# VectorE's part of a cached-attention decode kernel written as a loop over heads, with an alternating 0 or 1 in place of an odd/even branch

## The chip, the cores and the metric

One core of a Trainium2 chip. The metric is the device time of one execution in microseconds (us), the median of several runs. The engines are PE (TensorE), DVE (VectorE), ACT (ScalarE), POOL (GpSimd) and SP (SyncE); 16 DMA engines, over which the profile's page counts the shares of its queues, move the data. Three words are used throughout: a load *lands* when its data is complete; a *relay* is GpSimd waiting for a load and then raising a semaphore for another engine; the *chain* is the profile's path of work and waits followed back from the last instruction of the program.

## The reference, cut to what matters

One decode step: layernorm, attention of one query over a cache of 32768 keys for each of 32 heads, output projection, then a small MLP.

```
B, Sq, D = 1, 1, 640
H, Sk, Dh = 32, 32768, 192                       # k_cache, v_cache: bf16
q = (x @ wq).reshape(B, Sq, H, Dh)               # one row per head
scores = einsum("bhqd,bhkd->bhqk", q, k_cache) * Dh ** -0.5
o = einsum("bhqk,bhkd->bhqd", softmax(scores), v_cache)
h = x + o.reshape(B, Sq, H * Dh) @ wo
out = h + relu(layernorm(h) @ w1) @ w2
```

K and V together are 805 MB and are read once. Everything else is small.

## The kernel before

It has no scheduler: each engine's program is written out by hand. A class `Program` plans every semaphore count first, and then emits instructions and waits. SyncE issues the loads. A head's K and V come in four tiles each of 3072 KB; K tiles have four buffers, V tiles two.

```
for h in range(H):                                   # dma_program, on SyncE
    for ld in range(NL if h < LAST else NL - 1):
        load(kt[ld][:], rows(k_hd, h, ...), f"dk{ld}", "k", h, ld)
        if n >= NV:
            g.wait("PV", hp, 2 * lp + 1)             # the V tile two before is used up
        load(vt[ld % NV][:], rows(v_hd, h, ...), f"dv{ld % NV}", "v", h, ld)
        ...                                          # wq every 8 heads, wo every 2
```

PE computes most scores of a tile and the value products; DVE computes the scores of 28 of every 64 rows of a partition by multiplying and reducing, and normalizes each head. PE and ACT already execute heads 1 to 30 as a loop (their semaphores are counted down by one head's amount at the end of a turn, so that a turn's waits are constants). DVE's program is written out for all heads, because odd and even heads differ:

```
def o_scale(g, h):                                   # head h goes to row h % 2 of the pair
    g.wait("PV", h, len(chunks(h)) - 1)
    g.wait("rec", h)
    g.do(lambda: dve.tensor_scalar_mul(out=o_pair[:, :, h % 2, :], in0=o_ps[...], scalar1=rec[0:2, 1:2]), ...)

def o_turned(g, h):                                  # only an odd head's oT (the pair) is projected
    g.wait("oT", h)
    if h % 2 == 1:
        g.do(lambda: dve.tensor_copy(out=oT[:], in_=mm[:, 0:3]), "dve_pe", ("oTc", h))
    else:
        g.do(lambda: dve.memset(oT[:], 0.0), "dve_pe", ("oTc", h))

for h in range(H):                                   # dve_program
    for c in range(len(chunks(h))):
        scores_dve(g, h, c)
        if c == 0 and h > 0:
            den_rec(g, h - 1)
            o_scale(g, h - 1)
        if c == 1 and h > 0:
            o_turned(g, h - 1)
```

The softmax here doesn't subtract the row's maximum and nothing guards it: scores larger than these inputs give would overflow.

## Time and profile before

| | before |
|---|---|
| time, median | 1926.88 us of 3 runs |
| data read | 824.97 MB |
| instructions built for DVE / GpSimd | 981 / 352 |

The prediction below shows the lines on which it rests. The row of data rates is to be read beside them, one number for each fortieth of the span, in GB/s:

```profile
GB/s 408 430 432 433 433 432 432 433 433 431 433 430 433 433 433 433 433 432 427 434 433 433 433 431 433 430 435 432 430 431 431 435 432 433 431 431 429 431 432 321
```

The rate is flat, at 427 to 435, from the second slice to the last but one.

### The profile page before, as it was taken

To read this page: it belongs to the slowest core of one execution; us is meant where nothing else is said; L and a number is where in the kernel's file an instruction comes from. 1 tells how busy PE (TensorE), PEld (TensorE's weight loads), DVE (VectorE), ACT (ScalarE), POOL (GpSimd) and SP (SyncE) were. 2 spreads that over 40 slices of the span, in tenths; PEclk is the share of its full clock that TensorE was granted. 3 is DMA by queue.
4 is the path that set the end of the run, shared out by engine and by line. 5 is a ranking of instruction groups with operands and counts; after the bars stand their busy time and mean duration, and the time that the engine had idled before them with its cause. 6 is when DMAs were issued, how large, how long until landed. Compare 5 with 4: busy or idle time off the path is not lost.

```text
span 1925.6 us, 36082 instructions
## 1 busy us (share of the span) xinstructions
PE 1563.4 (81%) x15899; PEld 1074.8 (56%) x15899; DVE 1546.3 (80%) x670; ACT 970.6 (50%) x2031; POOL 0.7 (0%) x6
## 2 busy tenths in 40 slices
PE   5887888787887888788788878888778888888788
PEld 4555555555555555555555555555555555555555
DVE  5888888787887888887788878888778887888786
ACT  4554555454554554555454554545445454545554
POOL 0000000000000000000000000000000000000000
PEclk8889888888989898888888888888888888898888
DMA  9999999999999999999999999999999999999997
GB/s 408 430 432 433 433 432 432 433 433 431 433 430 433 433 433 433 433 432 427 434 433 433 433 431 433 430 435 432 430 431 431 435 432 433 431 431 429 431 432 321
DMA packets 44799, 825.31 MB, mean 429 GB/s; under 512 B 4580, under 2 KB 6116, under 8 KB 12132
## 3 DMA queue, kind: packets, MB, share of 16 engines
q1 hardware_dynamic: 44762, 824.99, 99.8%
q8 instruction: 12, 0.20, 0.0%
q14 instruction: 15, 0.12, 0.0%
q10 hardware_dynamic: 10, 0.00, 0.0%
HBM read 824.97 MB, written 0.00 MB: 428 GB/s over the span
## 4 chain that ended last, share of the span: by engine, by line
DMA 76%; PE 22%; SPq 1%; issue 0%; ACT 0%; POOLq 0%; DVE 0%
DMA kt<-in_A_k_cache_dram 76%; PE o_ps L319 11%; PE tp L338 10%; SPq L221 1%; PE mm L319 1%; PE sp L319 0%; PE attT L319 0%; ACT kT L533 0%; POOLq L301 0%; DVE o_pair L631 0%; ACT pB L539 0%; PE mm L522 0%; ACT h1T L595 0%; DVE y_row L699 0%; DVE h_col L681 0%
## 5 line engine op out<-in xcount | busy, mean ns | idle before, releaser
L617 DVE TENSOR_TENSOR pr<-kt,qb 128x2304 f32<-128x2304 bf16 (+2 forms) x257 | 755.8, 2941 | 298.9 <-DMA kt<-in_A_k_cache_dram 282.6
L533 ACT COPY kT<-tp 128x1024 bf16<-128x1024 bf16 (+1 forms) x899 | 818.9, 992 | 342.2 <-PE tp L338 340.2
L338 PE MATMUL tp<-ident_f,kt 128*128 128x128 f32 x3459 | 571.7, 332 | 341.8 <-POOLq L301 341.8
L620 DVE TENSOR_REDUCE sc<-pr 128x12 f32<-128x2304 f32 (+2 forms) x257 | 755.3, 2939 | 8.9
L338 PEld LDWEIGHTS tp<-ident_f,kt 128*128 128x128 f32 x3459 | 498.1, 173 | 358.7 <-POOLq L301 357.5
L319 PE MATMUL o_ps<-vt,pB 128*2 128x384 bf16 x2286 | 470.9, 357 | 3.5 <-POOLq L301 3.4
L319 PE MATMUL o_ps<-vt,pA 128*2 128x384 bf16 x1778 | 331.0, 326 | 0.0
L319 PEld LDWEIGHTS o_ps<-vt,pB 128*2 128x2 bf16 x2286 | 184.1, 89 | 239.8 <-issue 87.6
L539 ACT ACTIVATE pB<-sp 128x20 bf16<-128x20 f32 (+2 forms) x258 | 47.9, 186 | 503.1 <-PE sp L319 503.1
L319 PEld LDWEIGHTS sp<-qm,kT 128*128 128x128 bf16 x6918 | 193.2, 97 | 77.7 <-issue 67.5
L319 PEld LDWEIGHTS o_ps<-vt,pA 128*2 128x2 bf16 x1778 | 151.0, 85 | 144.7 <-issue 8.1
L319 PE MATMUL sp<-qm,kT 128*128 128x2 bf16 x6918 | 212.0, 164 | 3.0 <-ACT kT L533 2.1
L548 ACT ACTIVATE pA<-sc 128x12 bf16<-128x12 f32 (+2 forms) x257 | 53.4, 208 | 89.0 <-DVEq L64 88.3
L539 ACT ACTIVATION_READ_ACCUMULATOR pB<-sp 128x1 f32 x258 | 50.2, 195 | 0.0
L548 ACT ACTIVATION_READ_ACCUMULATOR pA<-sc 128x1 f32 x257 | 48.7, 190 | 0.0
L625 DVE TENSOR_REDUCE rec<-mm 128x1 f32<-128x20 f32 x32 | 5.7, 179 | 51.6 <-PE mm L319 51.1
L319 PE MATMUL mm<-wq_s,xn_ln 128*1 (+1 forms) x160 | 18.7, 248 | 3.6 <-POOLq L301 3.6
L631 DVE TENSOR_SCALAR o_pair<-o_ps,rec 2x384 bf16<-2x384 f32 x32 | 19.4, 605 | 2.8 <-PE o_ps L319 1.7
L319 PE MATMUL attT<-oT,wo_s 128*128 128x1 bf16 x465 | 15.9, 163 | 0.3 <-DVE oT L638 0.3
L319 PEld LDWEIGHTS mm<-dsums,ones_mat 128*128 128x128 f32 x64 | 9.5, 188 | 10.7 <-issue 9.3
L319 PE MATMUL mm<-ones_row,row_e 1*128 1x1 bf16 x384 | 14.0, 159 | 0.0
L319 PEld LDWEIGHTS attT<-oT,wo_s 128*128 128x128 bf16 x465 | 13.8, 95 | 0.3 <-DVE oT L638 0.3
(69 smaller groups left out, 129.1 us busy)
## 6 DMA issues: line engine op xcount, KB each, us to landing
kt<-in_A_k_cache_dram SPq DMA_DIRECT2D x127, 3072.0 KB, 22.5
vt<-in_A_v_cache_dram SPq DMA_DIRECT2D x127, 3072.0 KB, 15.5
wq_s<-in_A_wq_dram SPq DMA_DIRECT2D x4, 1920.0 KB, 21.9
wo_s<-in_A_wo_dram SPq DMA_DIRECT2D x16, 480.0 KB, 16.3
kt<-in_A_k_cache_dram SPq DMA_DIRECT2D x1, 1920.0 KB, 19.7
kt<-in_A_v_cache_dram SPq DMA_DIRECT2D x2, 960.0 KB, 24.3
kt<-in_B_w_dram SPq DMA_DIRECT2D x1, 1920.0 KB, 18.3
wq_s<-in_B_w_dram SPq DMA_DIRECT2D x1, 960.0 KB, 20.3
```

Source lines behind the costliest of these rows:

```text
L221: g.do(lambda: nc.sync.dma_start(out=dst, in_=src), sem, label, by=16)
L319: return lambda: pe.matmul(o, lhsT=w, rhs=r, **kw)
L338: calls.append(lambda b=b, o=o: pe.transpose(out=dst[:, b, :], in_=src[:, o:o + 2 * P].bitcast(f32), identity=ident_f[:]))
L533: g.do(lambda: act.copy(out=kT[c % 2][:, b0:b0 + nb, :], in_=src[:, 0:nb, :].bitcast(bf16)), "act_pe", ("cp", h, c, k))
L539: g.do(lambda: act.activation(out=pB[c % 4][:, 0:jp], in_=sp[:, 0:jp], func=F.Exp, scale=SCALE, accum_out=dsums[:, 2 * c + 1:2 * c + 2]), ...
L548: g.do(lambda: act.activation(out=pA[c % 4][:, 0:jd], in_=sc[c % NC][:, 0:jd], func=F.Exp, scale=SCALE, accum_out=dsums[:, 2 * c:2 * c + 1 ...
L617: g.chain(lambda: dve.tensor_tensor(out=pr[:, 0:j1 - j0, :], in0=src[:, (off + j0) * Dh:(off + j1) * Dh].rearrange("p (j d) -> p j d", d=D ...
L620: g.chain(lambda: dve.reduce_sum(out=sc[c % NC][:, j0:j1], in_=pr[:, 0:j1 - j0, :], axis=X), "dve")
L625: g.chain(lambda: dve.reduce_sum(out=rec[:, 0:1], in_=mm[:, 0:2 * NCM], axis=X), "dve")
L631: g.do(lambda: dve.tensor_scalar_mul(out=o_pair[:, :, h % 2, :], in0=o_ps[0:2, 0:2 * Dh].rearrange("q (i d) -> q i d", i=2), scalar1=rec[0 ...
```

## The change

Its intent: VectorE, too, runs heads 1 to 30 as one loop. For that all heads must be alike. The new head always goes to row 1 of the pair, the old row 1 is copied to row 0 afterwards, and oT is always written, scaled by `odd`, which flips between 0 and 1. To count waits per turn, DVE no longer waits on a DMA's semaphore or on PE's general one: GpSimd relays each K tile to DVE as well, and PE counts what DVE waits for on a semaphore of its own. The core of the diff:

```diff
-        g.wait("k", h, ld)
+        if h == LAST and ld >= NL - 1:
+            g.wait("k", h, ld)
+        else:
+            g.wait("atd", "k", h, ld)
...
                 relay(g, "k", h, ld)
+                g.do(lambda: nc.gpsimd.sem_inc(sems["pool_dve"], 1))
+                book_relay(g, "k", h, ld, sem="pool_dve")
...
-        g.do(lambda: dve.tensor_scalar_mul(out=o_pair[:, :, h % 2, :],
+        g.do(lambda: dve.tensor_scalar_mul(out=o_pair[:, :, 1, :],
...
     def o_turned(g, h):
+        g.chain(lambda: dve.tensor_scalar(out=odd[:], in0=odd[:], scalar1=-1.0, scalar2=1.0, op0=A.mult, op1=A.add),
+                "dve", ("odd", h))
         g.wait("oT", h)
-        if h % 2 == 1:
-            g.do(lambda: dve.tensor_copy(out=oT[:], in_=mm[:, 0:3]), "dve_pe", ("oTc", h))
-        else:
-            g.do(lambda: dve.memset(oT[:], 0.0), "dve_pe", ("oTc", h))
+        g.wait("odd", h)
+        g.do(lambda: dve.tensor_scalar_mul(out=oT[:], in0=mm[:, 0:3], scalar1=odd[:]), "dve_pe", ("oTc", h))
+        if h < LAST:
+            g.chain(lambda: dve.tensor_copy(out=o_pair[:, :, 0, :], in_=o_pair[:, :, 1, :]), "dve")
...
-            dve_program(Program(book, sems, nc.vector))
+            looped("dve", nc.vector)
```

More of the change, by code (lines that the diff above doesn't have):

```diff
@@ L26, in __init__ @@
         self.log = []
-        self.links = 0
+        self.links = {}
     def wait(self, *label):
@@ L46, in chain @@
     def chain(self, fn, sem, label=None):
-        if self.links > 0:
-            self.wait("link", sem, self.links)
-        self.links += 1
+        n = self.links.get(sem, 0)
+        if n > 0:
+            self.wait("link", sem, n)
+        self.links[sem] = n + 1
         self.row = sem
-        self.do(fn, sem, ("link", sem, self.links))
+        self.do(fn, sem, ("link", sem, n + 1))
         if label is not None and self.planning:
-            self.book["at"][label] = self.book["at"]["link", sem, self.links]
+            self.book["at"][label] = self.book["at"]["link", sem, n + 1]
     def tell(self, sem, label):
-        self.wait("link", self.row, self.links)
+        self.wait("link", self.row, self.links[self.row])
         if self.planning:
@@ L175 @@
     oT = sbuf("oT", [P, 3], bf16)
+    odd = sbuf("odd", [P, 1], f32)
     x_col = sbuf("x_col", [P, DT], f32)
@@ L208, in v_tile @@
         return v_at[(h, ld)] if (h, ld) in v_at else vt[ld % NV][:]
-    names = ["pool_pe", "act_pe", "dve_pe", "act_dve", "dve_act", "dve", "pool_dve", "pool_act", "pe_act", "pe"]
+    names = ["pool_pe", "act_pe", "dve_pe", "act_dve", "dve_act", "dve", "dve_row", "pe_dve", "pool_row", "pool_dve", "pool_act", "pe_act", "pe"]
     names += [f"dk{i}" for i in range(NL)] + [f"dv{i}" for i in range(NV)] + ["dwq", "dwo", "dx", "dout"]
@@ L214 @@
     sems = {n: nc.alloc_semaphore(n) for n in names}
-    TAKEN = {"pe": ("pool_pe", "act_pe", "dve_pe"), "act": ("pe_act", "dve_act")}
+    TAKEN = {"pe": ("pool_pe", "act_pe", "dve_pe"), "act": ("pe_act", "dve_act"),
+             "dve": ("pool_dve", "act_dve", "pe_dve", "dve")}
     def dma_program(g):
@@ L278, in pool_program @@
         g.do(lambda: e.affine_select(out=ident_b[:], in_=ident_b[:], compare_op=A.not_equal, fill=1.0, base=0,
-                                     pattern=[[-1, P]], channel_multiplier=1), "pool_dve", ("ident",))
+                                     pattern=[[-1, P]], channel_multiplier=1), "pool_row", ("ident",))
         g.wait("x")
@@ L302, in relay, with book_relay @@
         book_relay(g, *label)
-    def book_relay(g, *label):
+    def book_relay(g, *label, sem="pool_pe"):
         if g.planning:
-            n = g.book["count"].get("pool_pe", 0) + 1
-            g.book["count"]["pool_pe"] = n
-            g.book["at"][("at",) + label] = ("pool_pe", n)
+            n = g.book["count"].get(sem, 0) + 1
+            g.book["count"][sem] = n
+            g.book["at"][("at" if sem == "pool_pe" else "atd",) + label] = (sem, n)
     pe = nc.tensor
@@ L403, in den_mm @@
             g.wait("oTc", h - 1)
-        pe_group(g, [mmul(mm[:, 0:2 * NCM], ones_mat[:], dsums[:], start=True, stop=True)], ("den", h))
+        pe_group(g, [mmul(mm[:, 0:2 * NCM], ones_mat[:], dsums[:], start=True, stop=True)], ("den", h), "pe_dve")
     def o_turn(g, h):
@@ L410, in o_turn @@
         pe_group(g, [mmul(mm[:, b:b + 1], rows[i][:, b:2 * Dh:3], ident_b[0:2, i:i + 1],
-                          start=(i == 0), stop=(i == 1)) for b in range(3) for i in range(2)], ("oT", h))
+                          start=(i == 0), stop=(i == 1)) for b in range(3) for i in range(2)], ("oT", h), "pe_dve")
     def project(g, h):
@@ L463, in pe_norm @@
         g.wait("st", "ln1")
-        pe_group(g, [mmul(mm[:, 0:2], mean_mat[:], ln_t["ln1"]["st"][:], start=True, stop=True)], ("mean", "ln1"))
+        pe_group(g, [mmul(mm[:, 0:2], mean_mat[:], ln_t["ln1"]["st"][:], start=True, stop=True)], ("mean", "ln1"), "pe_dve")
     def pe_start(g):
@@ L469, in pe_start @@
         pe_group(g, [lambda: pe.transpose(out=mm[:, 0:4].bitcast(bf16)[:, 0:DT], in_=x_row[:],
-                                          identity=ident_b[0:DT, 0:DT])], ("xT",))
+                                          identity=ident_b[0:DT, 0:DT])], ("xT",), "pe_dve")
         pe_norm(g)
@@ L506, in pe_end @@
         g.wait("h_col")
-        pe_group(g, [mmul(mm[:, 0:1], mean_mat[:], st[:, 0:1], start=True, stop=True)], ("mean", "ln2"))
+        pe_group(g, [mmul(mm[:, 0:1], mean_mat[:], st[:, 0:1], start=True, stop=True)], ("mean", "ln2"), "pe_dve")
         g.wait("st", "ln2")
-        pe_group(g, [mmul(sp[:, 0:2], mean_mat[:], st[:], start=True, stop=True)], ("mean2",))
+        pe_group(g, [mmul(sp[:, 0:2], mean_mat[:], st[:], start=True, stop=True)], ("mean2",), "pe_dve")
         g.wait("xn", "ln2")
@@ L519, in pe_end @@
                               start=(f == 0 and n == 0), stop=(f == FT - 1 and n == DT - 1), skip_group_check=True)
-                         for f in range(f0, f1) for n in range(DT)], ("y", i))
+                         for f in range(f0, f1) for n in range(DT)], ("y", i), "pe_dve")
         g.wait("y_col")
-        pe_group(g, [lambda: pe.transpose(out=mm[0:DT, 0:P], in_=y_col[:], identity=ident_f[:])], ("yT",))
+        pe_group(g, [lambda: pe.transpose(out=mm[0:DT, 0:P], in_=y_col[:], identity=ident_f[:])], ("yT",), "pe_dve")
     act = nc.scalar
@@ L605, in scores_dve @@
             return
-        g.wait("k", h, ld)
+        if h == LAST and ld >= NL - 1:
+            g.wait("k", h, ld)
+        else:
+            g.wait("atd", "k", h, ld)
         if c == 0:
             g.wait("qb", h)
-            if h > 0:
-                g.wait("PV", h - 1, 1)
         if h == LAST and c >= NC:
@@ L628, in o_scale @@
     def o_scale(g, h):
-        g.wait("PV", h, len(chunks(h)) - 1)
+        if h == LAST:
+            g.wait("PV", h, NCM - 1)
         g.wait("rec", h)
-        g.do(lambda: dve.tensor_scalar_mul(out=o_pair[:, :, h % 2, :],
+        g.do(lambda: dve.tensor_scalar_mul(out=o_pair[:, :, 1, :],
                                            in0=o_ps[0:2, 0:2 * Dh].rearrange("q (i d) -> q i d", i=2),
@@ L635, in o_turned @@
     def o_turned(g, h):
+        g.chain(lambda: dve.tensor_scalar(out=odd[:], in0=odd[:], scalar1=-1.0, scalar2=1.0, op0=A.mult, op1=A.add),
+                "dve", ("odd", h))
         g.wait("oT", h)
-        if h % 2 == 1:
-            g.do(lambda: dve.tensor_copy(out=oT[:], in_=mm[:, 0:3]), "dve_pe", ("oTc", h))
-        else:
-            g.do(lambda: dve.memset(oT[:], 0.0), "dve_pe", ("oTc", h))
+        g.wait("odd", h)
+        g.do(lambda: dve.tensor_scalar_mul(out=oT[:], in0=mm[:, 0:3], scalar1=odd[:]), "dve_pe", ("oTc", h))
+        if h < LAST:
+            g.chain(lambda: dve.tensor_copy(out=o_pair[:, :, 0, :], in_=o_pair[:, :, 1, :]), "dve")
     def dve_norm(g, tag, col):
         t = ln_t[tag]
-        g.chain(lambda: dve.reduce_sum(out=t["st"][:, 0:1], in_=col[:], axis=X), "dve")
+        g.chain(lambda: dve.reduce_sum(out=t["st"][:, 0:1], in_=col[:], axis=X), "dve_row")
         g.chain(lambda: dve.scalar_tensor_tensor(out=t["sq"][:], in0=col[:], scalar=1.0, in1=col[:], op0=A.mult,
-                                              op1=A.mult, accum_out=t["st"][:, 1:2]), "dve", ("st", tag))
+                                              op1=A.mult, accum_out=t["st"][:, 1:2]), "dve_row", ("st", tag))
         g.wait("mean", tag)
-        g.chain(lambda: dve.tensor_copy(out=t["mv"][:], in_=mm[:, 0:2]), "dve")
+        g.chain(lambda: dve.tensor_copy(out=t["mv"][:], in_=mm[:, 0:2]), "dve_row")
         g.chain(lambda: dve.scalar_tensor_tensor(out=t["nv"][:], in0=t["mv"][:, 0:1], scalar=t["mv"][:, 0:1],
-                                              in1=t["mv"][:, 1:2], op0=A.mult, op1=A.subtract), "dve")
+                                              in1=t["mv"][:, 1:2], op0=A.mult, op1=A.subtract), "dve_row")
         g.tell("dve_act", ("nv", tag))
         g.wait("sd", tag)
-        g.chain(lambda: dve.reciprocal(out=t["rs"][:], in_=t["sd"][:]), "dve", ("rs", tag))
+        g.chain(lambda: dve.reciprocal(out=t["rs"][:], in_=t["sd"][:]), "dve_row", ("rs", tag))
         g.wait("rs", tag)
@@ L656, in dve_norm, with dve_start @@
                                        op0=A.subtract, op1=A.mult), "dve_pe", ("xn", tag))
-    def dve_program(g):
+    def dve_start(g):
         for t, v in ((ones_row, 1.0), (mean_mat, 1.0 / D), (eps_t, eps), (row_e, 0.0), (ones_mat, 1.0), (dsums, 0.0),
-                     (o_pair, 0.0), (zero5, 0.0), (oT, 0.0)):
-            g.chain(lambda: dve.memset(t[:], v), "dve")
+                     (o_pair, 0.0), (zero5, 0.0), (oT, 0.0), (odd, 1.0)):
+            g.chain(lambda: dve.memset(t[:], v), "dve_row")
         g.wait("ident")
@@ L664, in dve_program, with dve_head, dve_end @@
         g.wait("xT")
-        g.chain(lambda: dve.tensor_copy(out=x_col[:], in_=mm[:, 0:4].bitcast(bf16)[:, 0:DT]), "dve")
+        g.chain(lambda: dve.tensor_copy(out=x_col[:], in_=mm[:, 0:4].bitcast(bf16)[:, 0:DT]), "dve_row")
         dve_norm(g, "ln1", x_col)
-        for h in range(H):
-            for c in range(len(chunks(h))):
-                scores_dve(g, h, c)
-                if c == 0 and h > 0:
-                    den_rec(g, h - 1)
-                    o_scale(g, h - 1)
-                if c == 1 and h > 0:
-                    o_turned(g, h - 1)
+    def dve_head(g, h):
+        for c in range(len(chunks(h))):
+            scores_dve(g, h, c)
+            if c == 0 and h > 0:
+                den_rec(g, h - 1)
+                o_scale(g, h - 1)
+            if c == 1 and h > 0:
+                o_turned(g, h - 1)
+    def dve_end(g):
         h = LAST
+        dve_head(g, h)
         den_rec(g, h)
@@ L681, in dve_program @@
         g.chain(lambda: dve.scalar_tensor_tensor(out=h_col[:], in0=attT[:, 0:DT], scalar=1.0, in1=x_col[:], op0=A.mult,
-                                                 op1=A.add, accum_out=t["st"][:, 0:1]), "dve", ("h_col",))
+                                                 op1=A.add, accum_out=t["st"][:, 0:1]), "dve_row", ("h_col",))
         g.chain(lambda: dve.scalar_tensor_tensor(out=t["sq"][:], in0=h_col[:], scalar=1.0, in1=h_col[:], op0=A.mult,
-                                                 op1=A.mult, accum_out=t["st"][:, 1:2]), "dve", ("st", "ln2"))
+                                                 op1=A.mult, accum_out=t["st"][:, 1:2]), "dve_row", ("st", "ln2"))
         g.wait("mean", "ln2")
@@ L688, in dve_program @@
         g.wait("mean2")
-        g.chain(lambda: dve.tensor_copy(out=t["mv"][:], in_=sp[:, 0:2]), "dve")
+        g.chain(lambda: dve.tensor_copy(out=t["mv"][:], in_=sp[:, 0:2]), "dve_row")
         g.chain(lambda: dve.scalar_tensor_tensor(out=t["nv"][:], in0=t["mv"][:, 0:1], scalar=t["mv"][:, 0:1],
-                                                 in1=t["mv"][:, 1:2], op0=A.mult, op1=A.subtract), "dve")
+                                                 in1=t["mv"][:, 1:2], op0=A.mult, op1=A.subtract), "dve_row")
         g.tell("dve_act", ("nv", "ln2"))
         g.wait("sd", "ln2")
-        g.chain(lambda: dve.reciprocal(out=t["rs"][:], in_=t["sd"][:]), "dve")
+        g.chain(lambda: dve.reciprocal(out=t["rs"][:], in_=t["sd"][:]), "dve_row")
         g.tell("dve_act", ("rs", "ln2"))
@@ L698, in dve_program @@
         g.wait("yT")
-        g.do(lambda: dve.tensor_copy(out=y_row[:], in_=mm[0:DT, 0:P]), "dve", ("y_row",))
+        g.do(lambda: dve.tensor_copy(out=y_row[:], in_=mm[0:DT, 0:P]), "dve_row", ("y_row",))
     book = {"count": {}, "at": {}}
     plan = Program(book, sems)
-    for f in (dma_program, pool_program, dve_program):
+    for f in (dma_program, pool_program):
         f(plan)
-    parts = {"pe": (pe_start, pe_head, pe_end), "act": (act_start, act_head, act_end)}
-    logs = {}
+    parts = {"pe": (pe_start, pe_head, pe_end), "act": (act_start, act_head, act_end), "dve": (dve_start, dve_head, dve_end)}
+    logs, links = {}, {}
     for e, (start, head, end) in parts.items():
         logs[e] = []
+        plan = Program(book, sems)
         for h in range(LAST):
@@ L716 @@
         plan.log = []
+        links[e] = dict(plan.links)
         end(plan)
@@ L741, in take @@
         def take(amounts):
+            g.flush()
             for s, n in amounts.items():
@@ L756, in looped @@
             g.sub[s] = g.seen[s] = ends_at[e][LAST - 1][s]
+        g.links = dict(links[e])
         end(g)
```

## The prediction

Where it is cut, it told a figure or a rule that no trace or run of this case shows. Its sum came to 0.0 us: -0.1 for instructions no longer fetched, 0 in the body, 0 for the moved semaphores and +0.1 at the end. The working of the -0.1 is among the cuts. So are the sizes of the copy and of a turn's end, two terms of the "1.15 us a head" (the copy also of the "0.52 us net" and of the 10 to 20 us more of busy time); the terms that are left come to some 0.75 us (0.16 + 0.11 + five steps of 0.04 + 0.28). Rival A's size and a part of the grounds for the range are cut too, so that 1924.8 to 1929.2 no longer follows from what stands there.

> **What bounds the kernel now.** I read the page's head first (engine shares, the DMA row of the 40 slices, the queue table), then the chain that ended last.
>
> ```profile
> span 1925.6 us, 36082 instructions
> PE 1563.4 (81%) x15899; PEld 1074.8 (56%) x15899; DVE 1546.3 (80%) x670; ACT 970.6 (50%) x2031; POOL 0.7 (0%) x6
> ...
> q1 hardware_dynamic: 44762, 824.99, 99.8%
> q8 instruction: 12, 0.20, 0.0%
> q14 instruction: 15, 0.12, 0.0%
> ...
> DMA 76%; PE 22%; SPq 1%; issue 0%; ACT 0%; POOLq 0%; DVE 0%
> ```
>
> Queue q1, which carries the K and V caches, keeps the 16 DMA engines busy for 99.8% of the span. 824.99 MB over 1925.6 us is 428 GB/s, and the slices between the first and the last show 427 to 435. VectorE (DVE) is busy 80% of the span but has 0% of the chain. The chain does contain 22% of PE. That is no sign that PE limits: the chain follows one transfer back to the instruction that released its issue, and the time in which that transfer merely stood in the queue counts as DMA. So I asked for the chain in order of time around the middle, one head boundary:
>
> ```profile
> 881.38 24.02 DMA kt<-in_A_k_cache_dram
> 905.40 0.02 issue
> 905.43 0.03 POOLq L301
> 905.45 0.04 issue
> 905.50 2.62 PE tp L338 x15
> 908.12 3.55 PE o_ps L319 x16
> 911.67 0.34 PE mm L319 x2
> 912.02 0.02 SPq L221
> 912.03 0.04 issue
> 912.08 27.07 DMA kt<-in_A_k_cache_dram
> ```
>
> A K tile lands, GpSimd relays it to PE, PE transposes and finishes the values of the tile before, and that frees a V buffer, so that SyncE issues the next V and then the next K. The K issue takes 22.5 us (median, the table of DMA issues) to land. A 3072 KB transfer (3.146 MB) by itself takes 7.3 us at 432 GB/s. The V just ahead of it and the K itself account for 14.6 us, so 22.5 - 14.6 = **7.9 us** of other work is still in the queue when the release comes. That is the margin: a release that comes up to some 7.9 us later (my working from these numbers) leaves the DMA engines without a gap.
>
> The timeline of DVE over the first tile of a head says how much room DVE itself has:
>
> ```profile
> 905.43 2.56 DVE L617 TENSOR_TENSOR pr<-kt,qb 128x2304 f32<-128x2304 bf16 x1 [3.62 <-DMA kt<-in_A_k_cache_dram]
> 908.02 2.55 DVE L620 TENSOR_REDUCE sc<-pr 128x12 f32<-128x2304 f32 x1
> 912.04 0.18 DVE L625 TENSOR_REDUCE rec<-mm 128x1 f32<-128x20 f32 x1 [1.47 <-PE mm L319]
> 912.26 0.16 DVE L626 RECIPROCAL rec<-rec 128x1 f32<-128x1 f32 x1
> 912.45 0.60 DVE L631 TENSOR_SCALAR o_pair<-o_ps,rec 2x384 bf16<-2x384 f32 x1
> 912.99 3.34 DVE L617 TENSOR_TENSOR pr<-kt,qb 128x3072 f32<-128x3072 bf16 x1
> 916.36 3.35 DVE L620 TENSOR_REDUCE sc<-pr 128x16 f32<-128x3072 f32 x1
> 919.89 0.06 DVE L640 MEMSET oT<- 128x3 bf16 x1 [0.18 <-DVE sc L620]
> ```
>
> The first tile of a head occupies DVE from 905.43 to 919.95, which is 14.5 us; K tiles come every 2 x 7.3 = 14.6 us. So that tile has almost no slack. The three other tiles of a head need 2.56 + 2.55 + 3.36 + 3.35 = 11.8 us and have 2.5 us of waiting for the K load each (2.52 and 2.50 in the same timeline). Over the program DVE waits 282.6 us for K loads.
>
> [...] the middle slices show 430 to 435 GB/s, so there is nothing left to win in the steady state. [...] PE and ACT already loop over 30 heads in this kernel, and the two instruction queues show 12 + 15 = 27 packets in all, where one fetch per turn would be 60[...]. [...] the o_pair scaling here reads fp32 from PSUM and takes 0.605 us for 384 elements[...].
>
> **The change part by part.**
>
> *Removed: instructions to fetch.* In the built programs DVE's list falls from 981 instructions to 164 (waits and semaphore steps counted), and GpSimd's grows from 352 to 479, as it now tells DVE too of each K tile. That is 817 - 127 = 690 fewer[...]. That is the only term that touches the bound in the body.
>
> *Added on DVE, per head.* (1) The flip of odd, 128x1: a 128x1 reciprocal takes 0.163 us here, so 0.16. (2) Scaling oT by a per-partition operand in place of a cast (0.164) or a memset (0.061), alternately, mean 0.11: the slope of L617 is (3352 - 2558) / 768 = 1.03 ns per element, so the 384 elements of o_pair take 0.40 and its fixed part is 0.21; so some 0.22, added 0.11. (3) The copy of o_pair within SBUF, 2x384 bf16: at most the 0.605 of the PSUM form[...]. (4) The end of a turn: four semaphore decrements and the counter at about 0.04 each (the "issue" steps of the chain)[...]. (5) The hop through GpSimd, 0.03 + 0.04 us in the chain before each K tile, now paid by DVE too: 4 x 0.07 = 0.28. Sum about **1.15 us a head**, some 0.5 of it counted as busy. DVE's idle time is (1925.6 - 1546.3) / 32 = 11.9 us a head, so DVE stays under its budget of 58 to 60 us a head with ten to spare.
>
> *Where it falls.* Items 1 to 3 (0.52 us net) come after the first tile's last reduction, at the one place with no slack, so DVE starts the second tile up to 0.6 us late and has it back one tile later out of 2.5 us of waiting. The release that matters, the values of chunk 1, needs only that reduction, which stands before the new work: it moves by the 0.07 us hop. Even 0.6 us, or 1.15, is far inside the 7.9 us margin. **0 us** in the body.
>
> *Moved.* The semaphore for each engine pair (PE to DVE, DVE's own) changes what is counted, not what is waited for: the den matmul stands behind the last values in PE's order, so the dropped wait for them was implied. **0 us.**
>
> *On the path: the end.* After the last transfer the chain runs through DVE. From it:
>
> ```profile
> 1914.96 0.62 DVE o_pair L631
> 1915.57 0.05 issue
> 1915.62 0.32 PE mm L319 x6
> 1915.97 0.17 DVE oT L638
> ```
>
> The flip of odd goes into the 0.40 us between the end of o_pair and the start of oT, in which DVE only waits for PE, so its 0.16 us plus a self-wait fit. The oT step gets the pointer operand, 0.22 for 0.16: **+0.06**, with a second wait perhaps **+0.1 us**. At the start one more memset of about 0.06 us lies before work that is ready at 10.9 us (ACT's qm), while the first K lands at 15.5: 0.
>
> Sum: -0.1 + 0 + 0 + 0.1 = 0.0 us. The prediction is 1926.9 us.
>
> **The rivals.** *A: DVE stalls at every turn.* [...] It would fall at the head boundary, before the first tile, the one with no slack. [...] Against it: 27 packets with two engines looping, and a body of some 40 instructions. [...] *B: DVE becomes the bound.* That needs over 10 us more per head; I count 1.15. Then it would be +1% or more. I see no such cost, unless a self-decrement of a semaphore waits for something unseen. *C: the gain is real*, because unrolled instruction fetching disturbed the loads or starved DVE's sequencer. The queue table gives all instruction traffic 0.32 MB of 825, 0.04%, so at the very most 0.7 us, and DVE's own waits are for K loads. *D: the relay delays PE*, because GpSimd does one more step per K tile: PE's increment still comes first, so only the V relay is later, by some 0.04 us, long before V is needed.
>
> **Range and chances.** The three runs before span 1.0 us[...]. So 1924.8 to 1929.2 at 8 in 10. A move of 2% is 38.5 us, 1.2 us a head that must get past both the slack and the backlog: 1.5% for slower, 0.5% for faster.
>
> **What would show it.** Right: q1 again at 99 to 100% and the same GB/s in the slices; the K issues again about 22.5 us to landing; fewer instruction packets; DVE busy up by some 10 to 20 us, its waits for K loads down by some 15 to 45 us, the oT group all of one form at about 0.2 us x32[...]; DVE still at 0% of the chain. Wrong: a DVE gap at the first tile of every head of several us; K issues that land in under 20 us (the backlog gone); slices under 425 GB/s; or a longer stretch after 1894 us, where PE and DVE end the program, from a cost on that path that I have not seen.

## The result, and the profile after

The changed kernel takes **1924.14 us** (median of 4 runs, 1923.93 to 1924.36); the kernel before, in the same rounds, 1926.99 (4 runs, 1926.21 to 1927.18). The ratio is 0.9986, with a 95% interval from 0.9969 to 1.0003. A ratio here is the mean time of one kernel's fast runs over that of the other's of the same rounds, so it is not quite the ratio of the medians. The interval just includes 1, but the two sets of runs lie 1.85 us apart without touching. The later jobs repeat the gap: the 13 runs of the three kernels in which DVE loops and nothing is added outside the loop lie at 1923.63 to 1924.57 us, the 20 runs of the kernel before at 1926.13 to 1927.27. The prediction's point, no difference at all, is off by 2.8 us, and 1924.14 lies below its range of 1924.8 to 1929.2. So what gave 2.85 us?

The page of the changed kernel, the lines that answer to those shown of before:

```profile
span 1922.4 us, 36522 instructions
PE 1563.5 (81%) x15899; PEld 1073.1 (56%) x15899; DVE 1560.6 (81%) x734; ACT 970.7 (50%) x2031; POOL 0.7 (0%) x6
...
q1 hardware_dynamic: 44762, 824.99, 99.9%
q8 instruction: 12, 0.20, 0.0%
q14 instruction: 9, 0.07, 0.0%
...
DMA 76%; PE 21%; SPq 2%; issue 1%; ACT 0%; POOLq 0%; DVE 0%
```

DVE is busier, by 14.3 us, and still has no part in the chain. Queue q1 carries the same packets. What fell is the row of q14, one of the two queues that the page calls "instruction": 9 packets where there were 15, of 8192 bytes each.

The new work on DVE, by the listing of groups (count, busy us, mean ns of one, idle time before it):

```profile
L650 DVE COPY o_pair<-o_pair 2x384 bf16<-2x384 bf16 x31 | 7.4, 237 | 0.0
L648 DVE TENSOR_SCALAR oT<-mm,odd 128x3 bf16<-128x3 f32 x32 | 7.1, 223 | 3.9 <-PE mm L324 0.3
L644 DVE TENSOR_SCALAR odd<-odd 128x1 f32<-128x1 f32 x32 | 4.9, 153 | 4.6
```

Where in time the 2.85 us are is told by the chain in order of time. The last whole K tile of the program and its end, in the kernel before:

```profile
1864.26 22.41 DMA kt<-in_A_k_cache_dram
...
1886.77 3.46 PE tp L338 x15
...
1922.02 0.28 DVE y_row L699
```

and in the changed kernel:

```profile
1860.46 23.21 DMA kt<-in_A_k_cache_dram
...
1883.76 3.46 PE tp L343 x15
...
1918.77 0.28 DVE y_row L713
```

From the first transpose of that tile to the last DVE instruction both kernels take the same time, 1922.02 - 1886.77 = 35.25 us and 1918.77 - 1883.76 = 35.01 us. The tile itself lands 3.0 us earlier. The gain is made before it, in the stage where the data rate stood at 427 to 435 GB/s all along.

The trace keeps one more thing that no view above shows. Each load raises its semaphore 16 times; I read that as once for each of the 16 DMA engines, when it has done its part. Who waits for the load waits for the last of them: on the last whole K tile of the kernel before, DVE starts at 1886.70 us, 0.02 us after the 16th increment and 4.0 us after the median one. Taking those 16 times apart shows how far the last engine is behind the one before it, and behind the median of the 16. The record doesn't number the engines; that it is one and the same that stays last is inferred from its staying alone and from its place changing almost only in steps. In the table, "last - median" is in us, for the same load of both kernels; the last column is how much later that load has fully landed in the kernel before.

```
landing at (before)   before: last - median   after: last - median   before later by
      602 us                 0.69                   1.34                 -0.6
      632                    1.63                   1.35                  0.3
      860                    1.55                   1.25                  0.3
      905                    2.44                   1.26                  1.2
     1129                    2.15                   1.26                  1.1
     1175                    3.08                   1.20                  2.1
     1400                    2.98                   0.92                  1.9
     1445                    3.87                   0.88                  2.9
     1665                    3.73                   0.88                  2.8
     1695                    4.66                   0.88                  3.7
     1887 (last K tile)      4.00                   1.55                  3.0
```

In the kernel before, one DMA engine falls behind the others in five steps of 0.93 to 0.99 us from one load to the next. Over the next dozen loads it makes up 0.1 to 0.15 us of each, so that some 0.8 to 0.87 us stays; beyond that its distance to the changed kernel hardly moves between the steps. Packets of q14 stand at 619, 884, 1154, 1410 and 1675 us: one ahead of each step. Their distance, 256 to 270 us, is what DVE needs for some 131 to 138 instructions, at 981 / 32 = 30.7 a head and 60 us a head. That a packet carries about so many is my estimate from this spacing; at that count, the 1116 and 2232 instructions added below make 8 to 9 and 16 to 17 packets more.

The other ten packets of q14 (57, 100, 323, 364, 501, 1083, 1375, 1846, 1893 and 1917 us) are followed by no such step. Those at 100 and 364 us lie in the same spacing as the five; at that time no engine stands out (last and second to last within 0.25 us of each other), so I take their engine to have started ahead of the last. Those at 323, 501, 1083, 1375 and 1846 us fit no spacing of DVE's; the record doesn't say whose they are. In the changed kernel no q14 packet is at the five places, and the last engine's lag shrinks from 1.34 to 0.87 us at 1854 us. From 200 to 1813 us the median engine lands within 0.4 us of the same time in both kernels, and from 1820 us on 0.6 us later in the kernel before. So it is mostly not the sum that got faster; it is the last of the 16.

Together the kernel before goes from 0.5 us ahead, just before the first step, to 3.8 us behind at 1842 us: 4.3 us. The changed kernel gives 0.8 back before 1887 us, where packets of the other instruction queue, q8 (12 a run, of 16384 bytes, at 1858 and 1873 us here), run and its own last engine falls from 0.92 to 1.55 us behind the median. What is left is the 3.0 us. The kernel before has the same packets of q8 in this stretch: there the second-to-last engine falls from 0.65 to 2.08 us behind the median, and the last one stays at 4.0. If these packets are what costs the changed kernel 0.8 us here, the same cost is hidden there.

### The profile page after: what moved, and what is told of

It is laid out like the page before. It is cut to its first block, busy times and chain, and to the rows that moved or that the text cites. A ratio compares the mean times of both kernels' runs of the same rounds, so it can differ in the third digit from the quotient of the medians.

```text
span 1922.4 us, 36522 instructions
## 1 busy us (share of the span) xinstructions
PE 1563.5 (81%) x15899; PEld 1073.1 (56%) x15899; DVE 1560.6 (81%) x734; ACT 970.7 (50%) x2031; POOL 0.7 (0%) x6
## 3 DMA queue, kind: packets, MB, share of 16 engines
q1 hardware_dynamic: 44762, 824.99, 99.9%
## 4 chain that ended last, share of the span: by engine, by line
DMA 76%; PE 21%; SPq 2%; issue 1%; ACT 0%; POOLq 0%; DVE 0%
DMA kt<-in_A_k_cache_dram 76%; PE o_ps L324 11%; PE tp L343 10%; SPq L224 2%; PE sp L324 0%; PE attT L324 0%; ACT kT L538 0%; POOLq L306 0%; PE mm L324 0%; DVE o_pair L638 0%; ACT pB L544 0%; PE mm L527 0%; DVE y_row L713 0%; ACT h1T L600 0%; DVE oT L648 0%
## 5 line engine op out<-in xcount | busy, mean ns | idle before, releaser
L623 DVE TENSOR_TENSOR pr<-kt,qb 128x2304 f32<-128x2304 bf16 (+2 forms) x257 | 756.0, 2942 | 278.9 <-POOLq L290 261.5
## 6 DMA issues: line engine op xcount, KB each, us to landing
kt<-in_A_k_cache_dram SPq DMA_DIRECT2D x127, 3072.0 KB, 22.5
```

Of the source, the lines that this page charges most:

```text
L623: g.chain(lambda: dve.tensor_tensor(out=pr[:, 0:j1 - j0, :], in0=src[:, (off + j0) * Dh:(off + j1) * Dh].rearrange("p (j d) -> p j d", d=D ...
```

## The experiments

The theory after that: **each fetch of DVE instructions, 8 KB, occupies one DMA engine, always the same, for about 0.9 us; a load is complete only when its slowest engine is, so the program runs at the pace of that engine.** Rivals: the new waits, the relay or the new operations made the difference; or DVE's instructions themselves cost time, fetched or not.

The 16 landing times fit the theory in one more point: of a lag of 0.93 to 0.99 us only 0.1 to 0.15 is made good. That the other engines do not take over the lagging one's share is my reading of this; no run tests it, and none shows the order of packets within one engine.

### The changed kernel with DVE's loop written out

```diff
-            looped("dve", nc.vector)
+            g = Program(book, sems, nc.vector)
+            dve_start(g)
+            for h in range(LAST):
+                dve_head(g, h)
+            dve_end(g)
+            g.flush()
```

> The changed kernel with one part undone: VectorE's program is written out for all 32 heads again (1109 instructions built), all its new operations, waits, relay and semaphores kept. Theory (an instruction fetch of 8 KB holds up one DMA engine, and the slowest of the 16 sets the pace): some 8 fetches are back in the body, the landings of a load again spread by steps of about 0.87 us to 4 us or more, and the time is back at 1926.5 to 1928.5 us, or above. Rival (the new waits, relay or operations gave the gain): it stays at 1924.1.

Measured: 1927.53 us (5 runs, 1927.25 to 1927.74), beside 1926.4 for the kernel before in the same rounds. The whole gain is gone, and with 1109 instructions in place of 981 its median is 1.1 us above the kernel before (ratio 1.0005, interval 0.9992 to 1.0019, so that this last difference isn't clear of noise). Its page:

```profile
span 1925.6 us, 36337 instructions
...
q14 instruction: 17, 0.14, 0.0%
```

Every operation, wait and relay of the change is in this kernel. What it lacks is the loop. q14's count is back at 17, and the last engine falls back again in steps, to 4.7 us behind the median at 1799 us.

### The loop without the new arithmetic

DVE's loop takes two heads a turn, 15 turns, so that odd and even may differ as before; no flip, no copy.

```diff
-        with eng.Fori(0, LAST - 1) as i:
+        with eng.Fori(0, (LAST - 1) // 2 if e == "dve" else LAST - 1) as i:
...
+            if e == "dve":
+                head(g, 2)
+                take(step[e])
```

> The loop without the new arithmetic: VectorE loops 15 times over a pair of heads, with the kernel before's o_pair rows, and memset or cast of oT; no flip of odd, no copy of o_pair (186 instructions built). Theory: as fast as the changed kernel, 1923.5 to 1924.7 us, as the instructions to fetch are as few. Rival (the moved head and scaled oT matter): back toward 1927.

Measured: 1924.36 us (5 runs, 1924.10 to 1924.57), q14 again 9 packets. It was not run in the same rounds as the changed kernel; against the kernel before in its own rounds the pair loop gains 2.0 us and the changed kernel 2.85, ratios 0.9989 and 0.9986, whose intervals overlap. So no gain or loss of the moved head and the scaled oT shows, though they make DVE 14 us busier. This is the simpler way to the same time, and no run was clearly faster than both.

### The kernel before with instructions added that do nothing

36 or 72 semaphore steps a head on DVE, on a semaphore nobody waits for:

```diff
+                if c in (3, 5, 7) and h < LAST:
+                    for n_ in range(12):                          # 24 in the second kernel
+                        g.do(lambda: dve.sem_inc(sems["fill"], 1 - 2 * (n_ % 2)))
```

> The kernel before with 36 semaphore steps a head on VectorE (in three groups of 12, after the second chunk of the last three K tiles) that nobody waits for: 2097 instructions in place of 981, so about 9 more fetches of 8 KB. Theory: +0.87 us for each, some +7.6 us, 1933 to 1936 us. If a fetch cost only its bytes on one of 16 engines (0.30 us): +2.7, 1929.7. If its bytes were spread over all 16: +0.2, 1927.1. If the steps cost VectorE time and that mattered, VectorE's waits for K loads would be used up.

> As the run with 36, with 72 steps a head: 3213 instructions, some 17 more fetches than the kernel before. Theory: linear, some +15 us, 1940 to 1944 us. Bytes on one engine: +5.3, 1932. Bytes over all 16: +0.3.

Measured: 1936.79 us (4 runs, 1935.32 to 1937.05) and 1946.35 us (4 runs, 1944.98 to 1948.22), beside 1926.4. The queue rows, first with 36 and then with 72:

```profile
q14 instruction: 23, 0.19, 0.0%
```

```profile
q14 instruction: 32, 0.26, 0.0%
```

8 packets more than before cost 10.4 us, 17 more cost 20.0: 1.3 and 1.2 us each. From the kernel before on the growth is as straight as the theory had it, though steeper than the 0.87 expected, so both times lie above the ranges. The last engine's lag stops growing at 5 to 6 us behind the first; beyond that all engines fall back together (with 72 steps the median engine is 18 us later at the end than in the changed kernel, and the slices from 490 us on, but for the last, show 422 to 432 GB/s). Bytes explain it neither way: on 16 engines they would have cost 0.2 and 0.3 us, on one, at the 0.31 us that the trace gives such a packet, 2.5 and 5.3. DVE's waits for K loads did not shrink from the 282.6 us before, so it was not short of time; the rows of its first multiply, with 36 and with 72:

```profile
L617 DVE TENSOR_TENSOR pr<-kt,qb 128x2304 f32<-128x2304 bf16 (+2 forms) x257 | 755.9, 2941 | 309.5 <-DMA kt<-in_A_k_cache_dram 293.8
```

```profile
L617 DVE TENSOR_TENSOR pr<-kt,qb 128x2304 f32<-128x2304 bf16 (+2 forms) x257 | 755.8, 2941 | 325.3 <-DMA kt<-in_A_k_cache_dram 296.8
```

### The same added instructions inside the loop

> The control for the two filled runs: the same 36 semaphore steps a head on VectorE, but inside the changed kernel's loop, where they are executed as often and fetched once. Theory: no step costs anything by itself, so 1923.7 to 1925 us. Rival (the steps, not their fetches, slowed the filled kernels): some +10 us, 1934.

The edit is the one with 12 above, made in the changed kernel's `dve_head`, so that 36 steps a head are executed but fetched once. Measured: 1923.87 us (4 runs, 1923.63 to 1924.24), q14 10 packets. The same instructions that cost 10.4 us written out (on the kernel before) cost nothing in a loop (beside the changed kernel's 1924.14 in its own rounds). What costs is fetching them, not executing them.

### Added instructions on GpSimd, on SyncE, and on both

Eight steps behind each V relay (GpSimd), or eight before a load's second wait (SyncE), in the changed kernel; the third kernel has both.

```diff
                 relay(g, "v", h, ld)
+                for n_ in range(8 if h < LAST else 0):
+                    g.do(lambda: e.sem_inc(sems["fill"], 1 - 2 * (n_ % 2)))
```

> The changed kernel with 8 semaphore steps on GpSimd behind each V relay of heads 0 to 30 (1471 instructions in place of 479), some 8 more fetches, for GpSimd. Theory: a fetch holds up the one engine that carries it, whoever asks; after that engine's own slack (up to 2 us) each costs about 1 us: 1929 to 1933 us. Rival (only VectorE's fetches cost, because VectorE stalls): 1924.

> The changed kernel with 8 semaphore steps on SyncE before each second wait of a load of heads 0 to 30 (1302 instructions in place of 310), some 8 more fetches, for SyncE. Theory: as for GpSimd, 1929 to 1933 us[...]. Rival: 1924.

> Both fills at once, on GpSimd and on SyncE. If their fetches go to two different DMA engines, these fall behind side by side and the time is about that of the slower of the two single fills (1929 to 1933 us). If both go to one engine, or if every fetch holds up all 16, the costs add: 1936 to 1942 us.

Measured: 1926.78 (GpSimd), 1926.40 (SyncE) and 1926.84 us (both), 4 runs each, beside 1926.61 for the kernel before and 1924.14 for the changed kernel in its own rounds. The q14 rows of the three, in that order:

```profile
q14 instruction: 16, 0.13, 0.0%
```

```profile
q14 instruction: 17, 0.14, 0.0%
```

```profile
q14 instruction: 24, 0.20, 0.0%
```

Two readings. First, the size was missed: I expected 1929 to 1933. The steps of the last engine are 0.63 to 0.69 us for GpSimd and 0.69 to 0.73 for SyncE, where DVE's are 0.93 to 0.99, but the first two or three fetches make no step, and the next one a smaller one. I take it that the engine concerned starts ahead of the last; no run numbers the engines. Second, and more telling, **the costs do not add**: 15 packets more cost no more than 7 or 8 do. The landings say why, as last and second to last of the 16 engines, in us behind the median:

```
landing at      GpSimd: last, second   SyncE: last, second   both: last, second
   860 us           1.52   0.60            2.02   0.41           1.64   1.07
  1130              2.59   0.62            2.47   0.46           2.11   2.08
  1400              2.95   0.45            2.79   0.19           2.68   2.65
  1798              4.23   0.21            4.64   0.77           4.51   4.16
```

With one filled program, one engine falls behind alone (in the table the second stays within 0.8 us of the median). With two, two engines fall behind side by side, and the load waits for whichever is last. So the fetches of GpSimd and of SyncE go to two different DMA engines, each to its own. This rules out that such a fetch holds up all 16, and that only VectorE's own stalls cost: its program is the loop in all three.

### What stays open

Why a fetch of 8 KB delays its engine by 0.93 to 0.99 us for DVE and 0.63 to 0.73 us for GpSimd and SyncE, while its packet is recorded with a duration of 0.31 us. And why a fetch costs about 1.1 to 1.3 us, more than one step, once the lag has reached its limit. No run here takes these apart. That the 0.8 us that the changed kernel gives back at the end comes from q8's packets is argued from their place, and from an engine of the kernel before that falls back at the same packets; no run moves them. That a packet of q14 belongs to DVE is inferred from the spacing and from the runs that add or remove instructions.

## Why the prediction was right or wrong

- **What bounds the kernel: right, and not far enough.** The loads bound it, and DVE has no part in the chain in either kernel. But "nothing left to win in the steady state" was read from a sum over 16 engines. A load is done when the last one is done, and that one was up to 4.7 us behind the median.
- **The step that failed: "Removed: instructions to fetch", -0.1 us.** That it is the only term that touches the bound was right. The size was wrong because it divided the bytes by 432 GB/s, the rate of all 16 engines; the 6 packets of 8192 bytes that are gone from the page, 49 KB, come to 0.1 us in this way too. In the landings it is one engine that a fetch puts back: five of DVE's fetches put it back by 0.93 to 0.99 us each, of which some 0.8 to 0.87 stayed; by 1842 us that made 4.3 us between the kernels, of which 2.85 us arrive at the end. The term told as -0.1 us measured -2.85. The dose runs show the same in the other direction.
- **Rival C was the true one, and was dismissed by the same division.** "At the very most 0.7 us" took all instruction traffic at the rate of all engines. The rival named disturbed loads as a way, and the 0.04% of the bytes was not the measure of it.
- **Rival A, a stall in every turn: did not happen.** 30 turns of the loop, and q14 fell from 15 to 9 packets: this loop isn't fetched again at every turn.
- **The tile with no slack: right, though the stretch shown isn't typical.** There DVE waits 4.65 us for the next K tile, as a load of wq lies between, which comes every 8 heads; in the two heads after it the wait at this place is 0.15 us and none.
- **Rivals B and D: did not happen.** DVE is 81% busy; with DVE's relay in place the pair loop is as fast as any.
- **The costs on DVE: right for the operations, too low for the loop and the hop.** The flip takes 0.153 us (0.16 told), the oT scaling 0.223 (0.22), the copy 0.237 (at most 0.605); busy time is up 14.3 us (10 to 20), the waits for K tiles are down from 282.6 to 261.5 (15 to 45 less). All of it is hidden, as the pair loop without these operations shows. The end of a turn (item 4) takes 0.51 us in the trace of the changed kernel (median of 30): four semaphore decrements 0.093 us apart, where 0.04 was told, then the counter and the branch. With the hop through GpSimd (item 5) DVE starts 0.151 us after the K tiles that it waits for have landed, where it was 0.024 (medians of 102 and 104 tiles), so that it costs 0.13 and not 0.07.
- **The end: right.** oT takes 0.06 us more and the flip hides in the wait for PE; the stretch after the last whole K tile is equal within 0.24 us.
- **The chances: right in kind.** The result is within 2%; the range was too narrow below because it left no room for a term sized by the wrong denominator.
- **The signs of being right all came, and told nothing of this.** q1 is at 99.9%, the K issues take 22.5 us, DVE is at 0% of the chain. None of them looks at the last of the 16 engines.

## What to carry to other kernels

In a kernel whose data rate is flat, here at 427 to 435 GB/s, ask what each of the 16 engines has to do, not what they do together. Here a load was complete only with its last engine, up to 4.7 us behind the median, and a packet of 8 KB, 0.02 us at the rate of all 16, put one engine back by 0.63 to 0.99 us. The written-out instruction streams were such small transfers; the loop removed most of DVE's, and its 14 us of extra work cost nothing, as DVE, 81% busy, had idle time. To check, take the 16 increments of one load's semaphore apart, and look whether the last one drifts away from the rest.
